# Three fused layers on one core: all low weight parts of the experts on VectorE, with a new table of conversions and two transfers of a skipped block on another queue

## The chip, the cores and the metric

The kernel runs on one core of one Trainium2 chip. The metric is the device time of one execution in microseconds (us). The median of three runs of the kernel before is 585.15 us (583.89 to 586.19).

## The reference

Three layers follow one another, all in float32.

1. Attention over batch 2, 8 heads, 768 positions, head size 64. A position sees the first 8 positions and the last 96 ones; a slope per head times the distance is subtracted from the scores.
2. A mixture of 8 experts over the 1536 resulting tokens of 512 values. `argmax(x @ w_gate)` names one expert per token, and `out = gate_w * eom * (relu(x @ w1[e]) @ w2[e])`, with 512 to 1024 to 512 values.
3. A gated layer: `((x @ w_a) * (x @ w_b)) @ w_out`, with 512 to 1536 to 512 values.

## The kernel before

**Numbers in two parts.** Every product is made from operands that are split into a high and a low part of TensorE's own 32-bit format: high times high, high times low, low times high. So each tile of weights passes through the helper `split_to` (lines 117 to 127). ScalarE writes the high part (`A.copy(wh, st)`, line 123), and then either VectorE or GpSimd writes the low part (`wl = st - wh`, line 127). On GpSimd this is done in two halves of 512 columns, on VectorE in one instruction of 1024.

**Stages.** Attention comes first and takes the first 107 us or so; in it, the weights of expert 0 are already split. Then the eight experts run in order of size, expert k with room for `CAPS[k]` tokens (144, 288, 256, 224, 224, 208, 192, 176). Then comes the gated layer to the end.

**An expert.** TensorE does "up" for f = 0 to 7 (function `up`: tile `ps_h`, four weight tiles each) and "down" for d = 0 to 3 (function `down`: tile `ps_y`, eight half tiles each). After each f, ScalarE writes the high part of the hidden values (line 488) and copies the second half of the result out of PSUM (line 495), and VectorE adds the halves and writes the low part (lines 496, 497). "Down" needs the low parts of all eight f. PSUM has six buffers for these results, so TensorE can run some f ahead of ScalarE and VectorE.

**Ticks.** All other work is put between by `tick(i)`, called after f = i (i = 0 to 7) and twice in each d (i = 8 to 15). The order of the instructions on each engine is the order of these calls, written out by hand in tables:

```
RT1 = {1: 1, 4: 1, 9: 1, 10: 1, 12: 1, 13: 2}
WS = {1: G, 2: V, 5: G, 7: V, 9: G, 11: V, 13: V, 14: V}
YS = {(5, 13): 0, (5, 15): 1}
ST, TT = ((3, 4, 10), (8, 9, 13))
```

`WS` gives the eight ticks of an expert at which one weight tile of the next expert is split, and the engine of its low part (G is GpSimd, V is VectorE). I call these steps s0 to s7. A step (`wstep`, line 154) first puts loads on SyncE's queue so that three tiles are on their way or in use, and then calls `split_to`. The staging pool `stp` has three buffers, so the load of step n+3 waits until step n's low part is done. `ST` and `TT` say when the gathered tokens of the next expert are scaled (line 442, ScalarE) and transposed (`turn`, line 444: TensorE, then ScalarE and VectorE). `YS` splits the finished columns of the output for the gated layer. `CV` holds loads and conversions of the gated layer's weights, which come as 64-bit numbers: `cload` (a transfer into one of three buffers `st64`), `conv1` (two ScalarE instructions), `conv2` (three on VectorE, one on GpSimd, line 1004), `conv3` (one on ScalarE, one on GpSimd).

**The wide-mask block.** Between attention and the experts, `tc.If(nbad == 1, label="wide")` (line 851) holds a slow attention for masks that the fast one can't do (more than 32 global positions, or a window outside 1 to 97). With these inputs the flag is 0 and every engine branches over the block. Behind the branch the queues' engines run the semaphore instructions that stand in for the transfers left out.

Of the kernel before, what the change touches and what calls it, by code (L numbers as in the profile page):

```python
# [25 lines left out]
B, H, S, D = 2, 8, 768, 64  # L26
# [3 lines left out]
P = 128  # L30
# [17 lines left out]
def moe_block_kernel(ctx, tc, qd, kd, vd, kt, vn, nv, wg, wg2, we, wm, out):  # L48
    nc = tc.nc
    V, A, G, T = nc.vector, nc.scalar, nc.gpsimd, nc.tensor  # L50
# [8 lines left out]
    def iota(t, pattern, base=0, cm=0):  # L59
        G.iota(t, pattern=pattern, base=base, channel_multiplier=cm, allow_small_or_imprecise_dtypes=True)  # L60


    x_dram = dr.tile([NTOK, XW], F32, name="x_dram")
# [163 lines left out]
    def run(*gs):  # L227
        gs = list(gs)
        while gs:
            gs = [g for g in gs if next(g, run) is not run]  # L230
# [187 lines left out]
    def gate_a(x, ps_pool, ptag, sb_pool):  # L418
        ps = ps_pool.tile([P, 4, P], F32, tag=ptag, bufs=2, name="ps_xt")
        for k in range(4):  # L420
            T.transpose(ps[:, k, :], x[:, k * P:(k + 1) * P], ident)
        xs = sb_pool.tile([P, 4, P], F32, tag="xT", bufs=2, name="xT")
        A.copy(xs, ps)
        return xs

    def gate_b(xs, t, ps_pool, ptag, bufs):
        pg = ps_pool.tile([P, 16], F32, tag=ptag, bufs=bufs, name="ps_g")
        for k in range(4):
            T.matmul(pg, xs[:, k, :], wg_sb[:, k, :], start=(k == 0), stop=(k == 3))
        V.tensor_copy(lg[:, t, :], pg)  # L430
# [85 lines left out]
    with ExitStack() as att:  # L516
# [238 lines left out]
        for n in range(nu + 3):  # L755
            for f in RS.get(n, ()):
                f()
            if n < nu:
                b, p, m = units[n]
# [91 lines left out]
    with tc.If(nbad == 1, label="wide"):  # L851
        qh = qd.rearrange("u (j d) s -> (u j) d s", j=2)
        with ExitStack() as fs:
            fp = fs.enter_context(tc.tile_pool(name="fp", bufs=1, side="left"))
            slope = fp.tile([P, 2], F32, name="slope")
            for b in range(B):
                V.memset(slope[:, 0:1], -0.5)
                with tc.For_i(0, H, 1) as h:
                    kf = fp.tile([64, S], F32, tag="kf", name="kf")
                    qf = fp.tile([64, S], F32, tag="qf", name="qf")  # L860
                    vf = fp.tile([P, QT, D], F32, tag="vf", name="vf")
                    nc.sync.dma_start(kf, kt[ds(h + b * H, 1)].rearrange("o p n -> (o p) n"))
                    nc.sync.dma_start(qf, qh[ds(h + b * H, 1)].rearrange("o p n -> (o p) n"))
                    nc.sync.dma_start(vf, vn[ds(h + b * H, 1)].rearrange("o (c p) d -> p (o c) d", p=P))
                    for i in range(QT):
                        fr = fp.tile([P, S], F32, tag="fr", name="fr")
                        fl = fp.tile([P, S], F32, tag="fl", name="fl")
                        fg = fp.tile([P, S], F32, tag="fg", name="fg")
                        fk = fp.tile([P, S], F32, tag="fk", name="fk")
                        fsc = fp.tile([P, S], F32, tag="fs", name="fsc")  # L870
                        iota(fr, [[-1, S]], base=i * P, cm=1)
                        iota(fg, [[1, S]])

                        V.tensor_scalar(fl, fr, 0.0, None, ALU.is_ge)
                        V.scalar_tensor_tensor(fl, fr, nl_f, fl, ALU.is_lt, ALU.mult)
                        V.tensor_scalar(fg, fg, ng_f, None, ALU.is_lt)
                        V.tensor_tensor(fk, fg, fl, ALU.max)
                        V.tensor_tensor(fg, fg, fl, ALU.is_gt)

                        V.scalar_tensor_tensor(fl, fr, -1.0, fr, ALU.mult, ALU.max)  # L880
                        V.tensor_scalar(fr, fg, -1.0, 1.0, ALU.mult, ALU.add)
                        V.tensor_tensor(fl, fl, fr, ALU.mult)
                        V.tensor_scalar(fg, fg, nl_f, None, ALU.mult)
                        V.tensor_tensor(fl, fl, fg, ALU.add)
                        V.tensor_scalar(fl, fl, slope[:, 0:1], None, ALU.mult)
                        for c in range(2):
                            pt = ps.tile([P, 384], F32, tag="h", bufs=6, name="ps_f")
                            T.matmul(pt, qf[:, i * P:(i + 1) * P], kf[:, c * 384:(c + 1) * 384], start=True, stop=True)
                            V.scalar_tensor_tensor(fsc[:, c * 384:(c + 1) * 384], pt, 0.125, fl[:, c * 384:(c + 1) * 384], ALU.mult, ALU.add)
                        V.tensor_tensor(fsc, fsc, fk, ALU.mult)  # L890
                        V.tensor_scalar(fk, fk, 1e9, -1e9, ALU.mult, ALU.add)
                        V.tensor_tensor(fsc, fsc, fk, ALU.add)
                        fm = fp.tile([P, 2], F32, tag="fm", name="fm")
                        V.tensor_reduce(fm[:, 0:1], fsc, axis=AX.X, op=ALU.max)
                        V.tensor_scalar(fm[:, 0:1], fm[:, 0:1], -1.0, None, ALU.mult)
                        A.activation(fsc, fsc, AF.Exp, bias=fm[:, 0:1])
                        V.tensor_reduce(fm[:, 1:2], fsc, axis=AX.X, op=ALU.add)
                        V.tensor_scalar(fm[:, 1:2], fm[:, 1:2], 1e-9, None, ALU.add)
                        V.reciprocal(fm[:, 1:2], fm[:, 1:2])
                        po = ps.tile([P, D], F32, tag="h", bufs=6, name="ps_fo")  # L900
                        for c in range(QT):
                            pt = ps.tile([P, P], F32, tag="x", bufs=2, name="ps_ft")
                            T.transpose(pt, fsc[:, c * P:(c + 1) * P], ident)
                            fT = fp.tile([P, P], F32, tag="fT", name="fT")
                            V.tensor_copy(fT, pt)
                            T.matmul(po, fT, vf[:, c, :], start=(c == 0), stop=(c == QT - 1))
                        fo = fp.tile([P, D], F32, tag="fo", name="fo")
                        V.tensor_scalar(fo, po, fm[:, 1:2], None, ALU.mult)
                        nc.sync.dma_start(x_dram[b * S + i * P:b * S + (i + 1) * P, ds(h * D, D)], fo)
                    V.tensor_scalar(slope[:, 0:1], slope[:, 0:1], 0.5, None, ALU.mult)  # L910
            for t_ in range(NT):
                fx = fp.tile([P, DM], F32, tag="fx", name="fx")
                nc.sync.dma_start(fx, x_dram[t_ * P:(t_ + 1) * P, 0:DM])
                gate_b(gate_a(fx, ps, "x", fp), t_, ps, "h", 6)
        run(r_expert(0, NT, lg, cells(ps, "h", 6)))
        run(r_factor(0, NT, lg, cells(ps, "h", 6)))
        run(r_rank(0, NT, cells(ps, "h", 6)))
        for a in (0, NT // 2):
            oh = []
            run(r_hot(a, a + NT // 2, oh))  # L920
            run(r_ids(oh, a + NT // 2, cells(ps, "h", 6)))
        V.memset(bn, 0.0)
        V.memset(caps[:, 0:1], -1.0)
        rb = r_control()
        for _ in range(RC0):
            next(rb)
# [99 lines left out]
    def ysplit(st, g, eng, yT):  # L1026
# [4 lines left out]
    rare, yq = [], []  # L1031

    RT1 = {1: 1, 4: 1, 9: 1, 10: 1, 12: 1, 13: 2}
    WS = {1: G, 2: V, 5: G, 7: V, 9: G, 11: V, 13: V, 14: V}

    YS = {(5, 13): 0, (5, 15): 1}
    ST, TT = ((3, 4, 10), (8, 9, 13))

    CV = {
        (3, 3): [(cload, nc.scalar)], (4, 1): [(cload, nc.scalar)],  # L1040
        (3, 10): [(conv1, (0, 0)), (conv2, (0, 0))], (4, 10): [(conv1, (0, 1)), (conv2, (0, 1))],
        (6, 1): [(conv3, (0, 0))], (6, 13): [(conv3, (0, 1))],
        (6, 4): [(cload, nc.scalar)], (6, 8): [(cload, nc.scalar)],
        (7, 8): [(conv1, (1, 0))], (7, 9): [(conv2, (1, 0))], (7, 10): [(conv1, (1, 1)), (cload, nc.sync)], (7, 11): [(conv2, (1, 1))],
        (6, 14): [(cload, nc.sync)], (7, 12): [(cload, nc.sync)],
        (7, 13): [(conv3, (1, 0)), (conv1, (12, 0))], (7, 15): [(conv3, (1, 1)), (conv1, (12, 1))],
    }
    for k, n in enumerate(CAPS):
        X = XT.pop(k)
# [9 lines left out]
        def tick(i):  # L1059
# [18 lines left out]
            for t_, (o, w) in enumerate(nxt):  # L1078
                if i == ST[t_]:
                    scale(gs[t_], w)  # L1080
                if i == TT[t_]:
                    if t_ == 0:
                        XT[k + 1] = xtiles(epp, CAPS[k + 1])
                    turn(gs[t_], XT[k + 1], o, w)
            if i in WS:
                wstep(WS[i])
            for f_, x in CV.get((k, i), ()):
# [4 lines left out]
            if k == 4 and i in (2, 3):  # L1092
                ygs[i - 2] = yload(0, i - 2, stage("st64"))
            if (k, i) in YS:
                ysplit(ygs.pop(YS[k, i]), YS[k, i], V, yT)

# [430 lines left out]
```

## Time and profile before

| | |
|---|---|
| median of 3 runs | 585.15 us (583.89 to 586.19) |
| the profiled execution's own time | 584.59 us |
| its span (first to last instruction) | 582.4 us |
| TensorE (PE) busy | 560.6 us, 96% |
| VectorE (DVE) busy | 408.9 us, 70% |
| ScalarE (ACT) busy | 306.8 us, 53% |
| GpSimd (POOL) busy | 274.4 us, 47% |
| granted clock of TensorE, mean | 0.999 |

Times in the trace count from the start of the span. [...] PEld is TensorE's loading of weights. SPq and ACTq are the transfer queues of SyncE and ScalarE. L127 is line 127 of the kernel.

### The profile page before, as it was taken

The page shows a single profiled execution, that of the slowest core. Times are in us where ns is not written, and L with a number is a line of the kernel's source. Part 1 is how long each engine was busy: PE and PEld are TensorE (multiplying, and loading weights), DVE is VectorE, ACT ScalarE, POOL GpSimd, SP SyncE. Part 2 cuts the span into 40 slices and gives each one's busy share as a digit, 9 for nine tenths or more (in the row PEclk, how much of TensorE's full clock was granted, in tenths as well). Part 3 has the DMA queues.
Part 4 walks back from the last instruction along what each step waited for, and adds up shares of the span by engine and source line. Part 5 has one row for each costly group of instructions (what it writes and reads, how often), then busy time and mean ns, then how long its engine had stood idle before and what let it go on. Part 6 is the DMA issues. An engine that isn't in the chain of part 4 may idle for free. (4 is left out here: it accounts for less than half of the span.)

```text
span 582.4 us, 10238 instructions
## 1 busy us (share of the span) xinstructions
PE 560.6 (96%) x3476; PEld 484.7 (83%) x3476; DVE 408.9 (70%) x975; ACT 306.8 (53%) x710; POOL 274.4 (47%) x264
## 2 busy tenths in 40 slices
PE   6999999989999999899999999999999999999995
PEld 4877777888999998899988788888888888888884
DVE  5879986646954777776857677676687686686563
ACT  5787774456746767667655466515424432442210
POOL 6534571654526373546253245625534545344325
PEclk9999999999999999999999999999999999999999
DMA  8686772348566888878760212230321312310014
GB/s 277 260 274 229 276 204 109 104 149 272 181 222 211 260 256 277 260 235 266 234 206 38 73 39 96 83 107 2 110 70 39 109 36 74 107 33 4 2 54 164
DMA packets 39551, 87.35 MB, mean 150 GB/s; under 512 B 6032, under 2 KB 17552, under 8 KB 39488
## 3 DMA queue, kind: packets, MB, share of 16 engines
q1 hardware_dynamic: 32544, 74.30, 38.8%
q0 software_dynamic: 2192, 6.95, 3.4%
q10 hardware_dynamic: 4752, 5.34, 2.9%
q8 instruction: 31, 0.51, 0.3%
q14 instruction: 32, 0.26, 0.1%
HBM read 73.33 MB, written 13.23 MB: 149 GB/s over the span
## 5 line engine op out<-in xcount | busy, mean ns | idle before, releaser
L127 POOL TENSOR_TENSOR wl<-st,wh 128x512 fp32r<-128x512 f32 x58 | 74.9, 1312 | 70.7 <-ACT wh L123 50.7
L1004 POOL TENSOR_TENSOR tx<-tx,st 128x512 int32<-128x512 int32 x36 | 52.4, 1469 | 93.0 <-DVE tx L1002 45.3
L123 ACT CAST wh<-st 128x1024 fp32r<-128x1024 f32 x56 | 59.3, 1058 | 30.8 <-DMA st<-we 30.3
L479 PE MATMUL ps_y<-h,wl 128*128 128x224 f32 (+7 forms) x288 | 74.1, 257 | 0.0
L475 PE MATMUL ps_y<-h,wh 128*128 128x448 f32 (+5 forms) x224 | 66.8, 365 | 3.8 <-DVE h L497 2.9
L127 DVE TENSOR_TENSOR wl<-st,wh 128x1024 fp32r<-128x1024 f32 x35 | 48.9, 1397 | 28.4 <-ACT wh L123 28.3
L479 PE MATMUL ps_h<-x,wl 128*128 128x224 f32 (+6 forms) x256 | 66.9, 261 | 0.0
L1300 PE MATMUL ps_o<-wh,gh 128*128 128x512 f32 x144 | 56.2, 390 | 0.9 <-ACT acc L1305 0.9
L617 ACT ACTIVATE pe<-pe,mx 128x256 f32<-128x256 f32 (+1 forms) x96 | 45.9, 479 | 21.0 <-DVE mx L613 21.0
L475 PE MATMUL ps_h<-x,wh 128*128 128x448 f32 (+4 forms) x192 | 56.3, 363 | 0.1
L1301 PE MATMUL ps_o<-wl,gh 128*128 128x512 f32 x144 | 56.1, 390 | 0.0
L1302 PE MATMUL ps_o<-wh,gl 128*128 128x512 f32 x144 | 56.1, 390 | 0.0
L1016 POOL TENSOR_TENSOR wl<-tx,wh 128x512 fp32r<-128x512 f32 x36 | 48.5, 1369 | 14.9 <-ACT wh L1015 14.9
L479 PEld LDWEIGHTS ps_y<-h,wl 128*128 128x128 f32 x288 | 55.1, 191 | 0.0
L1307 DVE TENSOR_TENSOR acc<-ps_o,acc 128x512 f32<-128x512 f32 x60 | 40.5, 689 | 19.8 <-PE ps_o L1302 19.4
L479 PEld LDWEIGHTS ps_h<-x,wl 128*128 128x128 f32 x256 | 49.0, 191 | 0.0
L1255 POOL TENSOR_TENSOR wl<-tt,wh 128x512 fp32r<-128x512 f32 x20 | 25.5, 1297 | 49.1 <-ACT wh L1253 49.1
L475 PEld LDWEIGHTS ps_y<-h,wh 128*128 128x128 f32 x224 | 42.1, 188 | 7.7 <-ACT hs L495 3.1
L613 DVE CUSTOM_DVE_ANT_0 pe<-ps_s,bias 128x256 f32<-128x256 f32 (+1 forms) x96 | 32.8, 398 | 11.2 <-PE ps_s L607 10.7
L475 PEld LDWEIGHTS ps_h<-x,wh 128*128 128x128 f32 x192 | 36.1, 188 | 1.7 <-DVE yt L507 0.3
L1253 ACT CAST wh<-tt 128x1024 fp32r<-128x1024 f32 x10 | 10.5, 1052 | 49.0 <-DVE tt L1248 49.0
L1112 PE MATMUL ps_ab<-Y2h,wh 128*128 128x512 f32 x88 | 34.3, 389 | 0.0
(339 smaller groups left out, 1507.4 us busy)
## 6 DMA issues: line engine op xcount, KB each, us to landing
st<-we SPq DMA_DIRECT2D x64, 512.0 KB, 4.7
st<-wm SPq DMA_DIRECT2D x32, 512.0 KB, 3.6
vc<-vd SPq DMA_DIRECT2D x16, 352.0 KB, 5.3
k<-kd SPq DMA_DIRECT2D x7, 464.0 KB, 5.9
y_dram<-zero SPq DMA_DIRECT2D x12, 256.0 KB, 6.4
x_dram<-x SPq DMA_DIRECT2D x6, 512.0 KB, 3.3
acc<-y_dram SPq DMA_DIRECT2D x6, 512.0 KB, 4.7
q<-qd SPq DMA_DIRECT2D x7, 384.0 KB, 6.0
```

Source lines behind the costliest of these rows:

```text
L123: A.copy(wh, st)
L127: eng.tensor_tensor(wl[:, r], st[:, r], wh[:, r].bitcast(F32), ALU.subtract)
L475: T.matmul(pt[:, 0:2 * n].rearrange("p (s n) -> p s n", s=2), a, M[:, k], start=(k == 0), stop=False)
L479: T.matmul(pt[:, 0:n], b, M[:, k, 0], start=False, stop=(k == last))
L617: A.activation(pe[:, t_, j, 0:n], pe[:, t_, j, 0:n], AF.Exp, bias=mx[:, t_, j:j + 1], scale=-1.0, accum_out=sm[:, t_, j:j + 1])
L1004: lambda t=txi, l=l: G.tensor_tensor(t, t, l, ALU.add)))
L1016: G.tensor_tensor(wl_, tx, wh.bitcast(F32), ALU.subtract)
L1112: T.matmul(pt, wh[:, k, :], yh[:, k, :], start=start and k == 0, stop=False, skip_group_check=more)
L1300: T.matmul(po, gh, wh, start=(i == 0), stop=False)
L1301: T.matmul(po, gh, wl, start=False, stop=False)
L1302: T.matmul(po, gl, wh, start=False, stop=(i == 1))
L1307: V.tensor_tensor(at, po, at, ALU.add)
```

## The change

Five tables are changed, and the queue of two transfers in the wide-mask block. `WS` has all eight steps on VectorE, at ticks 1, 2, 3, 7, 9, 11, 13, 14; `YS` and the third entry of `TT` come earlier; `CV` is rewritten. In the block, the load of v and the stores of the result are issued by ScalarE's queue. The number of loads, splits and conversions is the same.

```diff
-                    nc.sync.dma_start(vf, vn[ds(h + b * H, 1)].rearrange("o (c p) d -> p (o c) d", p=P))
+                    nc.scalar.dma_start(vf, vn[ds(h + b * H, 1)].rearrange("o (c p) d -> p (o c) d", p=P))
...
-                        nc.sync.dma_start(x_dram[b * S + i * P:b * S + (i + 1) * P, ds(h * D, D)], fo)
+                        nc.scalar.dma_start(x_dram[b * S + i * P:b * S + (i + 1) * P, ds(h * D, D)], fo)
...
-    WS = {1: G, 2: V, 5: G, 7: V, 9: G, 11: V, 13: V, 14: V}
-
-    YS = {(5, 13): 0, (5, 15): 1}
-    ST, TT = ((3, 4, 10), (8, 9, 13))
+    WS = {1: V, 2: V, 3: V, 7: V, 9: V, 11: V, 13: V, 14: V}
+
+    YS = {(5, 11): 0, (5, 13): 1}
+    ST, TT = (3, 4, 10), (8, 9, 12)
 
     CV = {
-        (3, 3): [(cload, nc.scalar)], (4, 1): [(cload, nc.scalar)],
-        (3, 10): [(conv1, (0, 0)), (conv2, (0, 0))], (4, 10): [(conv1, (0, 1)), (conv2, (0, 1))],
-        (6, 1): [(conv3, (0, 0))], (6, 13): [(conv3, (0, 1))],
-        (6, 4): [(cload, nc.scalar)], (6, 8): [(cload, nc.scalar)],
-        (7, 8): [(conv1, (1, 0))], (7, 9): [(conv2, (1, 0))], (7, 10): [(conv1, (1, 1)), (cload, nc.sync)], (7, 11): [(conv2, (1, 1))],
-        (6, 14): [(cload, nc.sync)], (7, 12): [(cload, nc.sync)],
-        (7, 13): [(conv3, (1, 0)), (conv1, (12, 0))], (7, 15): [(conv3, (1, 1)), (conv1, (12, 1))],
+        (3, 5): [(cload, nc.scalar)],
+        (3, 9): [(conv1, (0, 0))],
+        (3, 10): [(conv2, (0, 0))],
+        (4, 4): [(cload, nc.scalar)],
+        (4, 9): [(conv1, (0, 1))],
+        (4, 10): [(conv2, (0, 1))],
+        (6, 1): [(cload, nc.scalar)],
+        (6, 3): [(conv3, (0, 0))],
+        (6, 9): [(cload, nc.scalar)],
+        (6, 11): [(conv3, (0, 1))],
+        (6, 14): [(cload, nc.sync)],
+        (7, 4): [(conv1, (1, 0))],
+        (7, 7): [(cload, nc.sync), (conv2, (1, 0))],
+        (7, 8): [(conv1, (1, 1)), (conv2, (1, 1))],
+        (7, 9): [(conv1, (12, 0))],
+        (7, 11): [(cload, nc.sync)],
+        (7, 12): [(conv1, (12, 1))],
+        (7, 14): [(conv3, (1, 0)), (conv3, (1, 1))],
     }
```

## Rows read from the trace of the kernel before

**Rows 1.** The page's part 1: busy time, share and instructions of each engine.

```profile
PE 560.6 (96%) x3476; PEld 484.7 (83%) x3476; DVE 408.9 (70%) x975; ACT 306.8 (53%) x710; POOL 274.4 (47%) x264
```

**Rows 2.** Busy time by stretch: "up", then "down", of experts 0, 3, 4, 5, 6.

```profile
core 0: us, PE busy (x) PEld busy (x) DVE busy (x) ACT busy (x) POOL busy (x), PEclk, DMA share, GB/s
...
116.76:125.13 8.37, 8.22 (x67) 7.93 (x66) 1.87 (x6) 3.35 (x10) 2.27 (x4) 1.00 0.49 167
125.13:138.22 13.09, 10.03 (x76) 9.23 (x77) 8.33 (x18) 9.47 (x24) 8.73 (x7) 1.00 0.58 171
...
189.93:200.05 10.12, 10.12 (x66) 9.58 (x65) 7.61 (x15) 8.07 (x20) 3.26 (x3) 1.00 0.86 274
200.05:210.96 10.91, 10.91 (x75) 10.38 (x73) 9.88 (x15) 7.32 (x13) 7.12 (x6) 1.00 0.72 216
...
210.96:221.09 10.13, 10.13 (x66) 9.60 (x65) 7.16 (x15) 7.17 (x16) 5.56 (x4) 1.00 0.95 312
221.09:232.83 11.74, 11.34 (x74) 10.33 (x73) 8.52 (x15) 9.06 (x19) 5.44 (x5) 1.00 0.75 258
...
232.83:242.48 9.65, 9.65 (x67) 9.56 (x65) 6.90 (x12) 4.48 (x10) 7.43 (x5) 1.00 0.88 270
242.48:256.05 13.57, 11.51 (x75) 10.29 (x73) 9.75 (x18) 10.62 (x23) 7.54 (x6) 1.00 0.68 209
...
256.05:265.50 9.45, 9.34 (x66) 9.11 (x65) 7.91 (x13) 7.78 (x20) 3.14 (x3) 1.00 0.91 282
265.50:276.81 11.31, 10.74 (x75) 9.91 (x73) 7.04 (x16) 7.66 (x17) 6.68 (x5) 1.00 0.79 270
```

**Rows 3.** Busy time, the same columns: expert 7, and from there to the end.

```profile
276.81:294.24 17.43, 17.43 (x131) 17.43 (x129) 13.02 (x30) 10.71 (x30) 5.20 (x4) 1.00 0.73 229
294.24:582.40 288.16, 281.00 (x1238) 231.82 (x1236) 196.98 (x332) 113.02 (x190) 126.18 (x98) 1.00 0.21 71
```

**Rows 4.** Waits, 116.76 to 294.24 us: in total, times, longest.

```profile
SPq L137 <- POOL wl L127: 52.7, 21, 3.6
...
SPq L137 <- DVE wl L127: 20.7, 14, 2.3
...
ACT wh L123 <- DMA st<-we: 30.3, 23, 2.6
```

**Rows 5.** Timeline, expert 5: ScalarE, then TensorE; idle before and its releaser in brackets.

```profile
241.75 1.05 ACT L123 CAST wh<-st 128x1024 fp32r<-128x1024 f32 x1 [2.61 <-DMA st<-we]
...
243.93 0.66 PE L448 MATMUL ps_x<-ident,xs 128*128 128x128 f32 x4 [0.99 <-ACT xs L442]
...
247.75 0.43 PE L475 MATMUL ps_y<-h,wh 128*128 128x416 f32 x1 [0.76 <-DVE h L497]
```

**Rows 6.** Instructions on tiles wl and tb, all of the span: ns min/median/max.

```profile
L127 POOL TENSOR_TENSOR wl<-st,wh x58: 1262/1287/2339, 21.4 to 273.7; 128x512 fp32r<-128x512 f32 x58
...
L127 DVE TENSOR_TENSOR wl<-st,wh x35: 1209/1226/2247, 125.3 to 279.6; 128x1024 fp32r<-128x1024 f32 x35
...
L407 DVE TENSOR_SCALAR tb<-i,t_lo x12: 271/274/1332, 151.4 to 161.3; 128x128 f16<-128x128 f32 x12
```

**Rows 7.** Groups by line, VectorE, experts 4 to 6: busy, mean ns, idle before.

```profile
L127 DVE TENSOR_TENSOR wl<-st,wh 128x1024 fp32r<-128x1024 f32 x15 | 21.5, 1436 | 13.2 <-ACT wh L123 13.2
```

**Rows 8.** Timeline, expert 0: TensorE (end of f = 1), ScalarE, GpSimd, SyncE's queue.

```profile
118.66 0.23 PE L479 MATMUL ps_h<-x,wl 128*128 128x144 f32 x1
...
122.52 0.29 ACT L488 ACTIVATE h<-ps_h 128x144 fp32r<-128x144 f32 x1 [3.99 <-PE ps_h L479]
...
122.87 1.06 ACT L123 CAST wh<-st 128x1024 fp32r<-128x1024 f32 x1
...
131.31 1.05 ACT L123 CAST wh<-st 128x1024 fp32r<-128x1024 f32 x1 [2.12 <-DMA st<-we]
...
124.06 3.58 POOL L127 TENSOR_TENSOR wl<-st,wh 128x512 fp32r<-128x512 f32 x2 [5.36 <-ACT wh L123]
...
127.66 0.35 SPq L137 DMA_DIRECT2D st<-we  x1
```

**Rows 9.** Waits of SyncE's queue at the skipped block: in total, times, longest.

```profile
SPq L851 <- SPq L851: 2.0, 2, 1.5
```

## The prediction

> **What bounds the kernel now.** I read the page's busy times first. TensorE is busy 560.6 of 582.4 us, the other engines 70% or less [rows 1]. So only what TensorE stands idle for, or the length of its own work, can move the time, and the change leaves its matmuls alone. The table of stretches shows where it idles. From the end of expert 7 to the end it is busy 281.0 of 288.2 us, and the change hardly touches that stage [rows 3]. The experts are where there is something to win.
>
> "Up" and "down" of one expert are the same number of matmuls of the same length; "down" also holds the transposes of the next expert's tokens. Expert 3 shows no idle time in either, and its "down" is 10.91 - 10.12 = 0.79 us longer for eight transposes [rows 2]. By that measure "down" is too long by 11.74 - 10.13 - 0.79 = 0.8 us in expert 4, 13.57 - 9.65 - 0.79 = 3.1 us in expert 5, 11.31 - 9.45 - 0.79 = 1.1 us in expert 6, and in expert 0 (twelve transposes, 1.2 us) by 13.09 - 8.37 - 1.2 = 3.5 us [rows 2]. That is **8.5 us**, all that a better order can win here.
>
> The view of waits and the timeline say why. ScalarE takes its instructions in order, so a cast of weights that waits for its transfer holds up the hidden values behind it. ScalarE waited 30.3 us in 23 places for weight tiles; in expert 5 the cast of s1 came 2.61 us late, and TensorE then waited for the scaled tokens (0.99 us) and for low parts (0.76 us) [rows 4, 5]. The transfers are late because SyncE's queue waits for a staging buffer: 52.7 us in 21 waits for GpSimd's low parts, 20.7 us in 14 for VectorE's [rows 4]. 21 is every step that GpSimd has, three in each of seven experts.
>
> **The change, part by part.**
>
> *GpSimd's steps to VectorE.* Each GpSimd step is two instructions of 1.29 us, 2.6 us with what lies between, against 1.23 us on VectorE [rows 6]. A buffer comes free some 1.3 us sooner, three times in eight steps. Three buffers take turns, so each buffer's chain (load, cast, low part, next load) gets 3 x 1.3 / 3 = 1.3 us shorter per expert. There is a second gain. Beside GpSimd's work VectorE's instructions stretch: in experts 4 to 6 its steps took 1.44 us on average against a median of 1.23, and a 0.27 us instruction took up to 1.33 us [rows 6, 7]. Five VectorE steps per expert, three chains: 0.21 x 5 / 3 = 0.35 us more. Together 1.6 us per expert, 6.4 us over experts 3 to 6, where 5.0 us were lost. Two things keep me from taking all of it. The transfer engines are already busy 0.88 to 0.95 in the "up" stretches of experts 4 to 6, though only 0.68 to 0.79 in "down" [rows 2], so an earlier issue partly waits elsewhere. And VectorE gets fuller: expert 5 holds 6.90 + 9.75 = 16.65 us of it [rows 2]; three more steps make 20.3, less about 1.05 us that stretching costs (5 x 0.21), 19.3 us. That is 96% of the 20.1 us which expert 5 would last without waits. Bounds for experts 4 to 6: 5.0 us won at best; at worst the three steps are paid in full, 3 x 3 x 1.23 = 11 us lost. The supply is the nearer row, so I take 3.3 us won.
>
> *Steps at ticks 1, 2, 3 (before 1, 2, 5).* ScalarE casts (1.05 us) and VectorE subtracts three times in three ticks. In expert 5 a tick of "up" is 9.65 / 8 = 1.2 us [rows 2], so VectorE falls behind by about 3 x (1.15 + 0.7 - 1.2) = 2 us, an estimate from its rows with 0.7 us for the two hidden-value instructions. Ticks 4 to 6 hold no step and give 1.5 us back. So "down" finds it nearly caught up: no cost, unless s2's load is late. s2 now has five ticks since the step that frees its buffer (tick 14 of the expert before) instead of seven; s5 gets eight instead of six. I count these against each other. If the cover of ticks 4 to 6 is gone, the price is that of the slower rival.
>
> *Expert 0.* GpSimd's s0 lasted from 124.06 to 127.64 us (3.58 us, two halves) and the next load was issued at 127.66; its cast waited 2.12 us for it [rows 8]. On VectorE s0 ends at about 123.93 + 1.23 = 125.2, so that load starts 2.4 us sooner. The other delay there is larger: TensorE ended f = 1 at 118.9, but ScalarE's next instruction started only at 122.52, after 3.99 us idle [rows 8]. The profile puts that wait on TensorE, which had long been done; no data explains it. ScalarE had just jumped over the wide block, and 14 transfers added to its skipped code move where the code behind the jump lies. If the stop goes, most of the 3.5 us go; if it stays, about 1.4 us. I take 2.4, between the two.
>
> [...]
>
> *The skipped block.* Its transfers don't run. Behind the branch SyncE spent 2.0 us in two waits of stand-in instructions [rows 9], at a time when nothing waited for it; some of them now come to ScalarE, just ahead of scaling expert 0's tokens. Bounds: nothing, or some 8 stand-ins of under 0.1 us each; no row shows what one costs on ScalarE, and below nothing is excluded, since no work leaves it. I take 0.7 us, the upper end, because TensorE waits for that scaling.
>
> *YS, TT, CV.* The same splits and conversions at other ticks. The earlier third transpose (tick 12) concerns expert 0 alone. Expert 7 has no steps, and TensorE is busy for all of its 17.43 us [rows 3], so its conversions have cover; without that cover the last `conv3` would cost 1 to 2 us at the start of the gated layer. I take nothing. GpSimd, idle for more than half of the span [rows 1], loses 42 instructions; nothing waits for it.
>
> *The sum.* 3.3 + 2.4 - 0.7 = 5.0 us. The profiled execution took 584.59 us, so 579.6; the median of the runs lies 0.56 us above it. I say **580.1 us**.
>
> **The rivals.**
>
> *The supply gets faster, but the stop stays or returns at a place as dear.* For: no row shows what ended the stop. Then expert 0 wins 0.7 after the stand-ins' cost, and three casts behind a late ScalarE halve the rest: 1.7 + 0.7 = 2.4 us, 582.8.
>
> *The transfers themselves are the limit.* For: 0.95 busy in expert 4's "up" [rows 2]; a load issued earlier lands no earlier. Against: 0.68 in the "down" where expert 5 lost its time. Nothing is won but the shorter wait in expert 0, less the stand-ins: 584.5 to 585.5.
>
> *Slower: VectorE's and ScalarE's burst at tick 3 becomes the new wait.* The place is the third step of an expert. If its load lands after f = 3, ScalarE stands there with the hidden values of f = 4 to 7 behind it, which before went first. The price is a cast, a low part and the two instructions of a hidden value, 1.05 + 1.23 + 0.45 = 2.7 us, in experts 0, 4, 5, 6, less the 5.0 us won elsewhere, plus 1 us for a full VectorE: 11 - 5 + 1 = 7 us at most, and about 4.5 if one of the four escapes: 589.6. It decides from the point where s2's cast starts later than the end of f = 5. For: in expert 5 even s1 landed late [rows 5].
>
> **How the numbers follow.** A measurement of this kernel can tell about 0.5% from no change, 2.9 us, so faster means below 582.2. The forecast has a chance of 0.50 and a range of its own of 577 to 582; the stop that stays 0.22 (581 to 584.5); the transfers as limit 0.13; slower 0.15. Faster is nearly all of the first and a third of the second, 0.57; same is the rest of the second and the third, 0.28; slower 0.15. The range reaches down to 576, where almost all of the 8.5 us are won, and up to 586.5, which takes in the transfers' case and leaves out the slower one.
>
> **What would show it.** In the profile after, SyncE's waits for GpSimd at line 137 are gone, and those for VectorE have not taken their place in full. ScalarE's waits for weight tiles fall well below 30 us. "Down" of expert 5 is below 11.5 us and that of expert 0 below 11.5. VectorE is above 85% busy in expert 5, its steps near 1.23 us. ScalarE's 4 us stop after f = 0 of expert 0 is gone. I am wrong if "up" or "down" of an expert has grown and TensorE waits there for low parts, or if the stage from expert 7 on, 288.2 us, has changed by more than 1 us.

## The result, and the profile after

The kernel after takes **578.5 us** (median of 6 runs, 577.62 to 581.02) against 585.41 us before (6 runs, 583.89 to 586.89). The ratio is 0.9889, 95% interval [0.9864, 0.9914]: 1.1% faster. One run on record lies apart from all others, 693.76 us at a mean granted clock of 0.75 (the kernel "tables alone" below); its median and ratio leave it out. The forecast was 580.1 us, range 576 to 586.5. The number was right. Of the reasons, one was more right than I had dared to use, and the largest one was wrong.

The profiled execution took 578.40 us, its span is 576.7 us. The stretches of the kernel after follow; the columns are those of [rows 2], and the stretches are "up" and "down" of experts 0, 4, 5 and 6, then the stage from expert 7's end.

```profile
115.22:123.06 7.84, 7.84 (x66) 7.84 (x66) 5.36 (x11) 6.41 (x17) 1.68 (x3) 1.00 0.82 258
123.06:132.58 9.52, 9.39 (x79) 9.11 (x77) 8.48 (x18) 7.52 (x18) 4.53 (x3) 1.00 0.85 278
204.30:214.44 10.14, 10.14 (x67) 9.59 (x65) 8.51 (x15) 7.97 (x18) 2.60 (x2) 1.00 1.00 315
214.44:225.68 11.24, 11.12 (x75) 10.32 (x73) 9.96 (x20) 8.31 (x18) 1.65 (x1) 1.00 0.84 300
225.68:235.32 9.64, 9.64 (x66) 9.55 (x65) 8.35 (x14) 5.88 (x13) 4.43 (x4) 1.00 0.92 282
235.32:248.43 13.11, 11.31 (x74) 10.31 (x73) 11.63 (x19) 10.78 (x21) 1.69 (x1) 1.00 0.68 226
248.43:257.52 9.09, 9.09 (x66) 9.09 (x65) 7.13 (x14) 5.74 (x14) 0.00 (x0) 1.00 0.93 305
257.52:271.44 13.92, 12.27 (x74) 11.44 (x73) 11.23 (x19) 10.80 (x22) 3.00 (x2) 0.88 0.68 237
...
288.88:576.70 287.82, 280.99 (x1238) 231.72 (x1236) 197.95 (x332) 112.78 (x190) 126.94 (x98) 0.99 0.21 71
```

Against [rows 2, 3]: expert 0 fell from 21.46 to 17.36 us (-4.1). Experts 4 and 5 fell by 0.5 us each, but expert 6 grew from 20.76 to 23.01 (+2.25), so these three together *lost* 1.3 us. Expert 1 fell by 1.0 (27.89 to 26.88), the stage from expert 7's end by 0.3, and the first expert starts 1.5 us earlier. That last part can't be laid to the change: over all the profiles of this case, with the attention's code unchanged, the start lies between 115.1 and 117.7 us, and the kernels with the old and the new tables overlap there. With 0.5 us less outside the span this makes the 6.2 us between the two profiled executions.

The waits of ScalarE and of SyncE's queue, 115.22 to 288.88 us, columns as in [rows 4]:

```profile
SPq L137 <- DVE wl L127: 43.3, 17, 4.6
SPq L137 <- DVE ps_h L496: 32.2, 15, 5.1
SPq L137 <- DVE yt L507: 25.9, 13, 2.9
```
```profile
ACT wh L123 <- DMA st<-we: 19.9, 20, 2.6
```

SyncE no longer waits for GpSimd's low parts, but it waits as long for the buffers that VectorE holds (the lines for `ps_h` and `yt` are VectorE's work just ahead of a low part): all its waits at line 137 come to 125.2 us in the kernel before and 126.1 us in the kernel after. The timeline shows the rest, ScalarE at f = 1 of expert 0, then ScalarE and TensorE in expert 5 and in expert 6:

```profile
117.38 0.29 ACT L488 ACTIVATE h<-ps_h 128x144 fp32r<-128x144 f32 x1 [0.42 <-PE ps_h L479]
...
235.58 1.05 ACT L123 CAST wh<-st 128x1024 fp32r<-128x1024 f32 x1 [2.18 <-DMA st<-we]
...
238.74 0.43 PE L475 MATMUL ps_y<-h,wh 128*128 128x416 f32 x1 [1.62 <-ACT hs L495]
...
257.44 1.05 ACT L123 CAST wh<-st 128x1024 fp32r<-128x1024 f32 x1 [2.60 <-DMA st<-we]
...
260.57 0.41 PE L475 MATMUL ps_y<-h,wh 128*128 128x384 f32 x1 [1.32 <-ACT hs L495]
```

ScalarE's stop of 3.99 us in [rows 8] is gone. In experts 5 and 6 the third step, now at tick 3, stands and waits for its tile, with the hidden values of f = 4 to 7 behind it, and TensorE idles for one of them (`hs`). In expert 6 more follows: from 262.6 to 266.0 us the granted clock is 0.50, after TensorE had idled 1.32 us and then worked with gaps (0.17 and 0.16 us):

```profile
262.60:266.00 3.40, 3.26 (x12) 3.29 (x13) 3.40 (x6) 3.00 (x6) 0.25 (x1) 0.50 0.74 240
```

Half of 3.4 us, 1.7 us, is about what this stretch cost, an estimate: a pair of matmuls on `h` takes some 0.53 us in it and 0.29 us behind it.

### The profile page after: what moved, and what is told of

Same layout as the page of the kernel before. It is cut to its first block, busy times and chain, and to the rows that moved or that the text cites. A ratio compares the mean times of both kernels' runs of the same rounds, so it can differ in the third digit from the quotient of the medians.

```text
span 576.7 us, 10200 instructions
## 1 busy us (share of the span) xinstructions
PE 559.2 (97%) x3476; PEld 485.3 (84%) x3476; DVE 420.6 (73%) x996; ACT 308.2 (53%) x710; POOL 217.4 (38%) x222
## 5 line engine op out<-in xcount | busy, mean ns | idle before, releaser
L127 DVE TENSOR_TENSOR wl<-st,wh 128x1024 fp32r<-128x1024 f32 x56 | 70.9, 1267 | 19.3 <-ACT wh L123 18.6
L475 PE MATMUL ps_y<-h,wh 128*128 128x448 f32 (+5 forms) x224 | 68.1, 370 | 4.2 <-ACT hs L495 2.9
L123 ACT CAST wh<-st 128x1024 fp32r<-128x1024 f32 x56 | 59.2, 1057 | 21.0 <-DMA st<-we 19.9
L617 ACT ACTIVATE pe<-pe,mx 128x256 f32<-128x256 f32 (+1 forms) x96 | 45.9, 479 | 19.9 <-DVE mx L613 19.8
L435 POOL DMA_INDIRECT xs<-x_dram,idp_i x15 | 21.1, 1408 | 57.1 <-ACT wh L123 38.1
```

Source lines behind the costliest of these rows:

```text
L127: eng.tensor_tensor(wl[:, r], st[:, r], wh[:, r].bitcast(F32), ALU.subtract)
L475: T.matmul(pt[:, 0:2 * n].rearrange("p (s n) -> p s n", s=2), a, M[:, k], start=(k == 0), stop=False)
L617: A.activation(pe[:, t_, j, 0:n], pe[:, t_, j, 0:n], AF.Exp, bias=mx[:, t_, j:j + 1], scale=-1.0, accum_out=sm[:, t_, j:j + 1])
```

## The experiments

Two questions were open: which part of the change took ScalarE's stop away, and why 5 us that were there to be won in experts 4 to 6 were not won. This table holds all kernels: median and ratio to the kernel before, then from the profiled execution the length of expert 0, of expert 1, and of experts 4, 5 and 6 together, and the time at granted clock 0.50 within the experts. One profile stands for each kernel, so its parts need not add up to the difference of the medians.

| kernel | us | ratio [95%] | exp. 0 | exp. 1 | exp. 4 to 6 | at 0.50 |
|---|---|---|---|---|---|---|
| before | 585.41 | | 21.46 | 27.89 | 65.85 | 0 |
| after | 578.50 | 0.9889 [0.9864, 0.9914] | 17.36 | 26.88 | 67.14 | 3.41 |
| queues alone | 580.87 | 0.9929 [0.9895, 0.9963] | 17.74 | 27.95 | 66.19 | 3.41 |
| tables alone | 584.07 | 0.9992 [0.9956, 1.0028] | 21.57 | 26.89 | 65.13 | 6.82 |
| engines alone | 583.28 | 0.9975 [0.9950, 1.0001] | 23.09 | 26.89 | 64.56 | 10.24 |
| after, third step late | 579.42 | 0.9908 [0.9875, 0.9940] | 17.36 | 26.88 | 65.85 | 3.41 |
| before, 64 unexecuted | 579.59 | 0.9904 [0.9872, 0.9937] | 17.80 | 27.01 | 66.36 | 0 |
| before, 128 unexecuted | 579.71 | one run | 17.96 | 27.79 | 65.66 | 0 |
| before, 256 unexecuted | 580.40 | one run | 17.75 | 27.01 | 66.65 | 3.41 |
| before, two loads ahead | 582.26 | 0.9966 [0.9945, 0.9988] | 20.21 | 27.58 | 66.69 | 6.82 |
| after, y loads later | 582.13 | 0.9953 [0.9930, 0.9977] | 17.35 | 26.88 | 71.58 | 6.83 |
| the same, third step late | 580.55 | 0.9928 [0.9901, 0.9955] | 17.35 | 26.88 | 67.28 | 6.83 |
| after, four staging buffers | 573.71 | 0.9847 [0.9812, 0.9883] | 17.34 | 26.90 | 61.05 | 0 |
| before, 64 unexecuted, four staging buffers | 574.04 | 0.9830 [0.9809, 0.9851] | 17.10 | 26.90 | 62.39 | 0 |

The kernel before, in the same batches: 584.46, 584.18, 583.88 and 584.20 us.

### The parts of the change, one at a time

*The queues alone*: the kernel before with the two lines of the skipped block.

```diff
-                    nc.sync.dma_start(vf, vn[...]...)
+                    nc.scalar.dma_start(vf, vn[...]...)
...
-                        nc.sync.dma_start(x_dram[...], fo)
+                        nc.scalar.dma_start(x_dram[...], fo)
```

> The kernel before with the two transfers of the skipped block on ScalarE's queue, and nothing else. Theory: ScalarE's stop of 4.0 us behind the jump comes from where its code lies; it goes, expert 0 shrinks from 21.5 to 18 to 19 us, and the time falls by 2.5 to 3.5 us. Rival: VectorE's steps won expert 0 and the block's lines do nothing: the stop stays, expert 0 lasts 21.5 us, the time is within 1 us of before.

*The tables alone*: the kernel after with those two lines back on `nc.sync`.

> The changed kernel with the block's two transfers back on SyncE's queue. Theory: the stop of about 4 us is back, expert 0 lasts 19.5 to 20.5 us instead of 17.4, and the time is 2 to 3 us above the changed kernel's 578.5. Rival: the tables alone won it all: 578.5, expert 0 at 17.4 us.

*The engines alone*: the kernel before with VectorE for all steps, ticks as they were.

```diff
-    WS = {1: G, 2: V, 5: G, 7: V, 9: G, 11: V, 13: V, 14: V}
+    WS = {1: V, 2: V, 5: V, 7: V, 9: V, 11: V, 13: V, 14: V}
```

> The kernel before with all low parts on VectorE at the old ticks 1, 2, 5, 7, 9, 11, 13, 14, nothing else. Theory: buffers come free sooner; expert 5 falls from 23.2 to 20 to 21 us and expert 6 from 20.8 to 19 to 20, expert 0 by 1.4 us although the stop stays; 579 to 581 in all. Rival, the transfers themselves limit: experts 4 to 6 keep their 65.9 us within 1 us, 584 in all.

The two lines that move transfers which never run gave some two thirds of the gain by themselves (0.71 of 1.11%), and nearly all of what expert 0 won (21.46 to 17.74). The tables by themselves gave nothing that can be measured: the stop is back, 3.09 us long with the tables alone, 4.30 with the engines alone (first and second line).

```profile
121.58 0.29 ACT L488 ACTIVATE h<-ps_h 128x144 fp32r<-128x144 f32 x1 [3.09 <-PE ps_h L479]
```
```profile
121.78 0.29 ACT L488 ACTIVATE h<-ps_h 128x144 fp32r<-128x144 f32 x1 [4.30 <-PE ps_h L475]
```

Both kernels are dearer than expected. With the tables alone expert 0 takes 21.57 us instead of 19.5 to 20.5, 3.41 us of it at granted clock 0.50, and the time is 5.6 us above the kernel after instead of 2 to 3. With the engines alone expert 0 takes 23.09 us, 6.83 of it at 0.50, and expert 5 24.33 instead of 20 to 21.

The engines alone did what I had claimed for the supply and no more: ScalarE's waits for tiles in experts 4 to 6, 18.8 us in the kernel before, fall to 5.8. But in expert 5 another transfer is then late, the gathered tokens, and ScalarE stands there instead. The first two lines below are the view of waits of experts 4 to 6, kernel before and engines alone, the third the timeline of expert 5 with the engines alone:

```profile
ACT wh L123 <- DMA st<-we: 18.8, 11, 2.6
```
```profile
ACT wh L123 <- DMA st<-we: 5.8, 7, 1.8
```
```profile
240.30 0.72 ACT L442 ACTIVATE xs<-xs 128x512 f32<-128x512 f32 x1 [1.86 <-DMA xs<-x_dram,idp_i]
```

TensorE idles 1.6 us for a low part behind it, and 3.41 us at granted clock 0.50 follow, so that 1.3 us are left (65.85 to 64.56).

### Is it the queue, or where the code lies?

The kernel before with instructions that are never executed at the end of the skipped block; no transfer changes its queue.

```diff
+            for _ in range(64):
+                A.copy(slope[:, 1:2], slope[:, 0:1])
             for t_ in range(NT):
```

> The kernel before, with 64 ScalarE copies added at the end of the skipped wide-mask block; they are never executed, no transfer changes its queue. Theory (ScalarE's stop of some 4 us after its jump over the block hangs on where the code behind the jump lies, nothing else): moving the code by 64 instructions can take the stop away; then f = 1's hidden value of expert 0 starts near 118 us instead of 122.5, expert 0 lasts about 17.7 us instead of 21.5, and the time falls by 3 to 4 us. Rival (it was the queue of the two transfers and their stand-in instructions that mattered): the stop stays, expert 0 lasts 21.5 us, the time is the one of before.

> The kernel before, with 128 such copies that are never executed. Theory, if the position counts in steps of 128 instructions: the code behind the jump lies as it did before, the stop of some 4 us is back at the same place and expert 0 lasts 21 to 22 us. Rival (only that something moved counts, or another step): the stop is elsewhere or gone, expert 0 lasts under 19 us.

> The kernel before with 256 ScalarE copies in the skipped block that are never executed. [...]

With 64 copies the kernel before takes 579.59 us, as near to the kernel after as can be told (their intervals overlap): **code that never runs is worth what the whole change is**. ScalarE at f = 1 of expert 0, in the kernel before with 64 copies:

```profile
118.00 0.29 ACT L488 ACTIVATE h<-ps_h 128x144 fp32r<-128x144 f32 x1 [0.52 <-PE ps_h L479]
```

Steps of 128 instructions, the theory of the second of these runs, are not borne out: with 128 copies the stop, expected back, is gone, and with 256 it is gone too (ScalarE idles 0.51 us ahead of f = 1 in both). Of the positions tried, it stands only at that of the kernel before. The view of the DMA queues tells more. Each line is a queue with its packets, MB and share of the engines; first the kernel before from 121.0 to 121.4 us, then the kernel before with 64 copies from 113 to 124 us, where queue 14 has no packet at all:

```profile
q1 hardware_dynamic: 71, 0.03, 27.7%
q0 software_dynamic: 10, 0.02, 10.8%
q14 instruction: 1, 0.01, 4.8%
```
```profile
q1 hardware_dynamic: 998, 1.79, 49.6%
q0 software_dynamic: 192, 0.59, 16.6%
q8 instruction: 1, 0.02, 0.5%
```

In the kernel before, one packet of instructions (8 KB) comes in that window, and none on queue 14 from 113 to 121 us or from 121.4 to 122.5. ScalarE goes on at 122.52 [rows 8]. With the tables alone such a packet lies between 119.9 and 120.6 us and ScalarE goes on at 121.58; with the engines alone it lies there too, and ScalarE goes on at 121.78. The packets start at 121.01, 120.00 and 120.26 us, so the stop ends 1.5 to 1.6 us after a packet of instructions starts, however long it is. The packet comes about when expert 1's first three weight loads are through: in these three kernels the third landed at 120.8, 120.5 and 120.2.

The other kernels have the counterpart. ScalarE's branch over the block is at 110 to 112.3 us, and the stop stands 24 recorded instructions behind it in each kernel that has one. In the ten kernels without the stop, one packet of queue 14 comes right behind the branch, between 111.1 and 113 us; in the kernels with the stop none does. The line is the kernel after from 111.1 to 113 us; in the kernel before queue 14 has no packet from 110.4 to 121 us:

```profile
q14 instruction: 1, 0.01, 1.6%
```

So the packet comes ahead of the weight data in one case and about when they are through in the other. That it holds the code needed there is a guess; the next run tests it.

*Two loads ahead*: the kernel before, where the third load is issued by the first step.

```diff
-    wloads(3)
+    wloads(2)
```

> The kernel before with two of expert 1's weight loads put on SyncE's queue ahead of expert 0 instead of three; the third is issued by the first step, as later ones are. Theory (ScalarE's stop is its fetch of instructions, which in the kernel before was served at 121.01 us, only after the third weight load had landed at 120.79): the fetch is served when the second load has landed, near 118 us, the stop shrinks from 4.0 to 1 to 2.2 us and expert 0 lasts 18.5 to 20 us instead of 21.5. Rival (the fetch takes some 4 us wherever it stands): the stop stays at 3.5 us or more and expert 0 above 20.8 us.

ScalarE at f = 1 in this kernel, and its DMA queues from 119.8 to 120.4 us:

```profile
121.36 0.29 ACT L488 ACTIVATE h<-ps_h 128x144 fp32r<-128x144 f32 x1 [1.94 <-PE ps_h L479]
```
```profile
q0 software_dynamic: 13, 0.03, 12.5%
q14 instruction: 1, 0.01, 4.5%
```

The stop is 1.94 us instead of 3.99. Expert 0 lasts 20.21 us, 0.2 more than expected, with 1.9 us of it at granted clock 0.50, about 1 us lost; without those it would have been inside. So with one load fewer queued ahead about half of the stop is gone, and what is left ends 1.5 us after a packet again (it starts at 119.89). The packet did not come "when the second load has landed", as expected: that was at 118.6, and with the tables alone the packet comes 0.5 us before the third load has landed. What exactly it stands behind is therefore open. Whose packet it is the trace doesn't say; that a later one on queue 14 can come without a stop is seen with 256 copies (one between 119 and 120 us). That the stop hangs on where the code lies is shown (3.99 us, and gone with 64, 128 and 256 copies); that it is a fetch was not shown, the packets only point to it.

### Why experts 4 to 6 won nothing

*After, third step late*: tick 5 for the third step, as before the change.

```diff
-    WS = {1: V, 2: V, 3: V, 7: V, 9: V, 11: V, 13: V, 14: V}
+    WS = {1: V, 2: V, 5: V, 7: V, 9: V, 11: V, 13: V, 14: V}
```

> The changed kernel with the third step at tick 5 again instead of 3. Theory: ScalarE's wait of 2.6 us for the third step's tile, ahead of f = 4 to 7, is what made experts 5 and 6 lose time; they fall from 22.8 and 23.0 to 20 to 21 and 19 to 20 us, the granted clock stays at 1.00 in expert 6, and the time is 573 to 575 us. Rival: the loads are late in any order and the wait only moves to tick 5: experts 5 and 6 stay above 22 us, 578.

Expert 6 falls to 19.35 us, and expert 5 grows to 25.43. The late tile is only met at another place: 3.47 us of waiting in one go at a cast in expert 4. The rival, that the wait only moves, came nearer.

*After, y loads later*: two loads of 512 KB moved out of expert 4, where the transfer engines are busy for 1.00 of "up".

```diff
-    YS = {(5, 11): 0, (5, 13): 1}
+    YS = {(6, 4): 0, (6, 6): 1}
...
-            if k == 4 and i in (2, 3):
-                ygs[i - 2] = yload(0, i - 2, stage("st64"))
+            if k == 5 and i in (8, 9):
+                ygs[i - 8] = yload(0, i - 8, stage("st64"))
```

> The kernel after, with the two loads of finished output columns (512 KB each) moved from expert 4 (ticks 2, 3) to expert 5 (ticks 8, 9), and their splits to expert 6. Theory (expert 5's tiles come late because the transfer engines are full in expert 4): expert 5 falls from 22.75 to 20 to 21 us, ScalarE's wait at its third step from 2.2 to under 1 us, and no stretch at half clock follows in expert 5; the time is 1 to 2 us below the kernel after unless expert 6 takes the lateness over (then it stays at 23 us or more, and the time is the same). Rival (expert 5 is bound by VectorE or by the order of its steps): expert 5 stays above 22.5 us.

> The same as the run before it, with the third step at tick 5 instead of 3. Theory (transfers late plus the burst at tick 3 are the two losses left in experts 5 and 6): expert 5 at 20 to 21.5 us and expert 6 at 19 to 20 us, no stretch at half clock, 573 to 575.5 us. Rival (each loss moves on to the next expert): experts 4 to 6 together stay within 1.5 us of the kernel after's 67.1 us, and the time within 1.5 us of its 578.5.

Both missed. Expert 5 falls (21.46 and 21.21 us), but expert 6 takes 26.68 and 25.05 us, with 6.83 us at granted clock 0.50; in the first, expert 4, which the loads had left, grows too (23.44 us against 21.38), and why is open. The second run has the sum of its rival (67.28) and a time 2.0 us above the kernel after; the first is worse than any theory had it. In all kernels with three staging buffers experts 4 to 6 stay between 64.6 and 71.6 us: the order moves the lateness, it doesn't remove it.

*Four staging buffers*, in the kernel after, and in the kernel before with 64 unexecuted copies:

```diff
-        return (stp if name == "st" else pools["V"]).tile([P, 1024], F32, tag=name, bufs=3, name=name)
+        return (stp if name == "st" else pools["V"]).tile([P, 1024], F32, tag=name, bufs=4 if name == "st" else 3, name=name)
...
-    def wstep(eng, ahead=3):
+    def wstep(eng, ahead=4):
...
-        yt = pool.tile([P, w], F32, tag="yt", bufs=4, name="yt")[:, 0:n]
+        yt = pool.tile([P, w], F32, tag="yt", bufs=3, name="yt")[:, 0:n]
```

> The kernel after, with four staging buffers for the experts' weights instead of three (each load is issued one step sooner; one result buffer of down, yt, is given up for the room). Theory (what is left in experts 4 to 6 is the way round three buffers: a load of 5 to 7 us, cast, low part and the waits between, 8 times over 3 buffers, needs more than the 20.1 and 18.8 us that experts 5 and 6 would last): with a fourth buffer expert 5 falls to 20 to 20.8 us, expert 6 to 18.8 to 19.7, no stretch at half clock before the end, time 572 to 574.5 us. Rival (the transfer engines' own rate is the limit, 0.91 to 0.95 busy there): loads issued sooner only last longer, ScalarE's waits for tiles stay, experts 4 to 6 together stay above 65 us, time 577 us or more.

> The kernel before (its own tables, GpSimd's low parts included) with 64 unexecuted copies in the skipped block, so that ScalarE's stop is gone, and with the four staging buffers. Theory (engine of the low parts and the ticks matter little once the loads have room): experts 4 to 6 together 60 to 62 us and 573 to 575.5 us, within 1.5 us of the run before it. Rival (moving the low parts to VectorE is worth 3 us or more of its own in experts 4 to 6): 577 us or more, TensorE waits for GpSimd's low parts there.

Both came out as the theory said, but for 0.4 us in the second one's sum (62.39). Stretches "up" and "down" of experts 4, 5 and 6, kernel after with four buffers:

```profile
205.55:215.69 10.14, 10.14 (x67) 9.60 (x65) 9.02 (x17) 8.03 (x20) 1.96 (x2) 1.00 0.94 301
215.69:226.56 10.87, 10.87 (x75) 10.33 (x73) 9.43 (x17) 7.75 (x14) 2.17 (x1) 1.00 0.85 315
226.56:236.19 9.63, 9.63 (x66) 9.55 (x65) 8.88 (x15) 6.87 (x16) 3.92 (x3) 1.00 0.91 300
236.19:247.35 11.16, 10.99 (x74) 10.31 (x73) 10.60 (x19) 10.35 (x19) 0.95 (x1) 1.00 0.73 249
247.35:256.45 9.10, 9.10 (x67) 9.10 (x65) 8.65 (x16) 7.51 (x19) 1.09 (x1) 1.00 0.86 287
256.45:266.60 10.15, 10.15 (x74) 9.93 (x73) 9.52 (x17) 8.13 (x17) 2.16 (x2) 1.00 0.84 285
```

The transfer engines are about as busy as in the kernel after (0.73 to 0.94 of a stretch, there 0.68 to 1.00), and TensorE idles only 0.17 us in 61.05. The waits of ScalarE for tiles in experts 4 to 6, kernel after, then the two kernels with four buffers:

```profile
ACT wh L123 <- DMA st<-we: 14.8, 12, 2.6
```
```profile
ACT wh L123 <- DMA st<-we: 0.6, 1, 0.6
```
```profile
ACT wh L123 <- DMA st<-we: 4.2, 5, 1.5
```

So the transfer rate was no limit. What was short was the number of tiles under way: a load takes 4.8 us from issue to landing (the median in these experts, in the kernel before and in the kernel after), up to 7.9 in the kernel after, and three buffers leave no room for a late one. The two tiles that held up experts 5 and 6 of the kernel after took 6.8 and 6.4 us. The version with four is the fastest kernel here, 573.71 us (573.55 to 577.08; the kernel after 577.62 to 581.02). The two ran in different batches and the intervals of their ratios just overlap; what carries the reading are experts 4 to 6, 6.1 us shorter. The old tables come to 574.04 with it: the new tables, the engine of the low parts with them, are worth 62.39 - 61.05 = 1.3 us in experts 4 to 6 of one profile each, and nothing that the two medians can tell apart.

## Why the prediction was right, and where its steps were wrong

- **What bounds the kernel, 8.5 us to win: right.** Four buffers and no stop win 4.1 us in expert 0 (I had found 3.5) and 4.8 in experts 4 to 6 of the 5.0 that I found there.
- **Expert 0, 2.4 us: right in mechanism, mis-sized.** It gave 4.1. I had taken the middle between "the stop goes" and "it stays"; it went, as the kernel with 64 unexecuted copies shows by itself (-3.7). That I laid it to moved code and not to an engine's work is borne out. My 1.4 us for the case that the stop stays did not show: expert 0 then took 21.57 and 23.09 us, not 20.1. Without half of the 3.41 and 6.83 us at clock 0.50 it would be 19.9 and 19.7, an estimate. What the stop is, no run shows: a packet of instructions starts 1.5 to 1.6 us ahead of its end, but the stop is not at the branch, since ScalarE ran on for 24 recorded instructions and some 7 us behind it. With 128 and with 256 copies, one run each, it did not come back, and what other positions would do is open.
- **The supply, 3.3 us won in experts 4 to 6: wrong.** 1.3 us were lost. The step that failed is the one from a shorter way round the buffers ("1.6 us per expert, 6.4 us over experts 3 to 6") to less idle time on TensorE: the shorter way does shorten the waits (18.8 to 5.8 us with the engines alone), but shorter waits are not yet less idle time. With three buffers one late transfer still stops ScalarE (2.18 and 2.60 us in experts 5 and 6 of the kernel after), and the hidden values stand behind it. The loads, 4.8 us in the median, did not change; a fourth buffer was what they lacked, a cause that my rivals did not hold. "The transfers are the limit" gave the right sign for these experts by a wrong reason. A full VectorE (19.98 of 22.75 us in expert 5) was not the cause either: with four buffers it is busy 19.48 of 20.79 us there, and the expert is shorter.
- **Ticks 1, 2, 3, "no cost, unless s2's load is late": the exception came true.** I set the five ticks that s2 has against the eight of s5 and took nothing. It is s2 that came late, at 235.58 and 257.44. The rival "burst at tick 3" priced 2.7 us per expert in four experts. It decided in two: "down" of expert 5 is 13.11 - 9.64 - 0.79 = 2.7 us too long, and that of expert 6 by 13.92 - 9.09 - 0.79 = 4.0, of which 1.7 at the lower clock. But expert 5 had lost 3.1 before at another place, so the mechanism cost expert 6 alone. The run with the third step late shows that it is no price of the tick as such: there the loss goes to expert 5.
- **The skipped block's stand-ins, 0.7 us on ScalarE: wrong, it is 0.** No stand-in came to ScalarE: it runs one semaphore instruction of 17 ns at line 851 in the kernel before (first line) and in the kernel after (second), SyncE eight in both.

```profile
L851 ACTq EVENT_SEMAPHORE  x1: 17/17/17, 111.6 to 111.6; - x1
```
```profile
L851 ACTq EVENT_SEMAPHORE  x1: 17/17/17, 110.7 to 110.7; - x1
```

- **`YS`, `TT`, `CV`, nothing: right.** Expert 7 lasts 17.44 us (17.43 before), the rest 287.82 us (288.16).
- **Not foreseen: 1.0 us in expert 1.** It lasts 27.6 to 28.0 us in four kernels with GpSimd's parts, 26.9 in all without, and 26.9 to 27.0 in three that keep them. So GpSimd's parts alone don't decide it; it wasn't followed further.

Of the signs that I named, these came: no wait for GpSimd, ScalarE's waits at 19.9 us, "down" of expert 0 at 9.52, VectorE 88% busy in expert 5 (19.98 of 22.75), steps at 1.22 us, the stop gone, the rest unmoved. These did not: "down" of expert 5 is 13.11, not below 11.5, and expert 6's has grown, though TensorE waits there for hidden values more than for low parts; I had named that as a sign that I am wrong. And SyncE's waits for VectorE did take the place of those for GpSimd in full (125.2 and 126.1 us in all), but that says little: with four buffers, too, SyncE waits 44.7 us on `wl` where the kernel after has 43.3. The total was right in part by luck: an under-sized gain (+1.7), a start that happened to lie 1.5 us earlier, expert 1 (+1.0) and the 0.7 that was not paid made up for a supply that came out 4.6 below its term.

## What to carry to other kernels

A stop that no data explains, some instructions behind a jump (here 24, and 3.99 us), can hang on where the code lies. Try a few unexecuted instructions before crediting an edit with the gain (64 copies left 0.52 us of idle time there), look for a packet on the instruction queue (here 1.5 to 1.6 us ahead of the stop's end), and put a smaller stack of loads ahead of the jump (two loads instead of three left 1.94 us). That the packet is a fetch was not shown. Where an engine waits for tiles (ScalarE 14.8 us in experts 4 to 6 of the kernel after) although the transfer engines are not full on average (0.68 to 1.00 of a stretch there), count the buffers under way before moving steps about: one more buffer won here the 6.1 us in experts 4 to 6 that four orders of steps and loads (the kernel after and three variants of it) couldn't. And test each part of a change alone: here the part that looked idle carried the result.

## What was not expected of the hardware

- Instructions that never run are worth 4.6 us of 584.18 (64 copies), 3.7 of it in expert 0, through a stop of 3.1 to 4.3 us that three kernels show (1.9 us in the one with fewer loads ahead) and the others don't.
- TensorE's granted clock fell to 0.50 for 3.41 us at a time, 6.83 us in three kernels; nine of the fourteen kernels show it in the experts. Gaps in TensorE's work stood ahead of it: one of 1.32 us in the kernel after, one of 1.55 us with the third step late. A gap did not always bring it: in the kernel after, one of 1.62 us in expert 5 left the clock at 1.00, and the one of 1.32 us in expert 6 was followed by 0.50. What decides was not tried; the lesson is that a gap of 1.3 us went with a loss of 3 us here (with the 1.7 us estimated above).
